# Attention into a causal gated unit on one core: k^T v over 128 rows, wide fillers, 7-product output blocks for two more batches, and a new order

## The chip, the cores and the metric

The kernel runs on one core of a Trainium2 chip. The time is device microseconds of one execution. A profile is one execution recorded by the hardware profiler, as times of every instruction from the start of the span. The engines: PE multiplies matrices (PEld is its loading of weights, which lies beside it), DVE (VectorE), ACT (ScalarE) and POOL (GpSimd) work element by element, SP issues DMAs; ACT and POOL issue some too.

## What is computed

```python
# q, k, v: (8, 8, 576, 64) float32: batch, heads, tokens, head size
kv  = einsum('bhsd,bhse->bhde', k, v)
out = einsum('bhsd,bhde->bhse', q, kv)
out = out / sqrt(mean(out * out, axis=-1) + 1e-6) * g_norm
x   = out.transpose(0, 2, 1, 3).reshape(8, 576, 512)
gate_pre[t] = sum over i in 0..4 of conv_w[i] * x[t - 4 + i]     # zeros ahead of the first token
gate = 1 / (1 + exp(-gate_pre))
result = (gate * (x @ w_val)) @ w_out       # w_val, w_out: (512, 512); conv_w: (5, 512); all three float64
```

There is no softmax: a 64x64 matrix k^T v for each head is all that attention needs of k and v.

## The kernel before

Everything is float32, and PE makes two passes of each matmul. The eight batches run through the same steps, and the steps of neighbouring batches are interleaved. There is no loop around them: PLAN is a text of 1103 steps, each a function with its arguments, carried out from first to last when the program is built. Its order is therefore the order of every engine's own queue; an engine that waits holds up all that stands behind it in its queue.

The steps of a batch b:

- load_half (L290) loads half of the heads of k or v, 576 KB, as 128 partitions (s, the parity of the head, times 64 groups p of nine tokens), for two heads g each: nine tokens of 64 numbers in a row, 2304 contiguous bytes. Batch 0's v goes by ACT's queue, the rest by SP's; batch 1's lies in slots 1 and 2 of gv, which are free then; other batches have one buffer for each half. load_q (L300) loads a pair of heads as four DMAs of 32 partitions; batches 0 and 1 use load_q_rows (L309).
- kv_product (L417), a half at a time: nine tokens of the group x 2 heads r x 2 parities s, each a matmul of 64 rows (the groups) and 64 columns. Four of them, one for each of four heads, on the four quarters of the array, can be in flight. They collect in the two banks "raws", one for each s. kv_copy (L425) moves the sums onto the diagonal blocks of kv_bd.
- turn_q (DVE) or, for batches 0 and 1, turn_q_rows (PE, L451, tile qTps) and sort_q (ACT) transpose q. raw_product (L472) and raw_pair (L489, 64x64 products) multiply it with kv.
- square (ACT), sums (DVE, L515), powers (POOL, L521) and normalise (DVE for batch 0, else ACT, L533) make x; turn_x and keep_x, or from batch 2 turn_blocks (DVE, L561) and move_blocks (POOL's DMAs, L569), transpose it into xT; halo (POOL) copies the convolution's edge.
- gate_start (ACT), four gate_tap (DVE, L586) and gate_end (ACT) make the gate. x @ w_val is val_product (L598) for batches 0 and 1; from batch 2 it is val_fast (L648), seven products where eight would be needed, with x_sums (DVE) ahead of it and val_keep (ACT copies and DVE adds, L655 to L669) between. gated (DVE, L611) multiplies with the gate in place in gv, which has three slots, b modulo 3.
- The last product takes two batches at a time, i = b // 2. out_product i c (L679; L686 for the rest of both batches, c = 8) makes 128 tokens by 512 columns from four matmuls of 512 columns, and keep_out (ACT, L694) copies them. For i = 3 alone, two such blocks are one pair made of seven products of 2 matmuls by 256 columns: token_sums (DVE, L719), fast_product (L745), and fast_keep (four ACT copies, three DVE adds, L754 to L769). weight_sums (DVE, L702) prepares the weights for it once. store (L778) writes a block as four DMAs.
- narrow_weight turns float64 weights into float32, on DVE and ACT, eight steps a tile.

Buffers that set waits: PSUM has five banks "mm", one "tp" and two "raws"; val_fast takes three mm banks at once, a pair of fast_product two, an out_product one. Tile ot has three buffers, w64 (staged weights, later the token sums) three.

keep_warm (L408) is work for PE without use: matmuls of the identity with itself, 13 of them at the start and three at two places later.

Of the kernel before, what the change touches and what calls it, by code (L numbers as in the profile page):

```python
# [9 lines left out]
FP32 = mybir.dt.float32  # L10
# [5 lines left out]
P = 128  # L16
# [3 lines left out]
load_q_rows 0 1; stage_weight cw 0; load_q_rows 0 0; load_half v 0 0; load_half k 0 0; load_half v 0 1;  # L20
load_half k 0 1; warm_up; stage_weight wval 1; stage_weight wval 0; keep_warm 13; turn_q_rows 0 0;
turn_q_rows 0 1; sort_q 0 0; narrow_weight cw 0 0; turn_q_rows 0 2; sort_q 0 1; narrow_weight cw 0 1;
turn_q_rows 0 3; narrow_weight cw 0 2; narrow_weight cw 0 3; sort_q 0 2; turn_q_rows 0 4; narrow_weight cw 0 4;
kv_product 0 0; narrow_weight cw 0 5; sort_q 0 3; load_q_rows 1 0; narrow_weight cw 0 6; narrow_weight cw 0 7;
load_half k 1 0; sort_q 0 4; load_q_rows 1 1; load_half v 1 0; keep_warm 3; kv_product 0 1; load_half k 1 1;
stage_weight wval 2; keep_warm 3; turn_cw; load_half v 1 1; kv_copy 0; stage_weight wval 3; raw_product 0 3;
narrow_weight wval 0 0; raw_product 0 2; narrow_weight wval 1 0; square 0 3; keep_cw; narrow_weight wval 0 1;
raw_product 0 4; sums 0 3; raw_product 0 1; square 0 4; powers 0 3; square 0 2; narrow_weight wval 0 2;
raw_product 0 0; sums 0 2; narrow_weight wval 0 3; sums 0 4; powers 0 2; narrow_weight wval 1 1; normalise 0 3;
load_q 2 2; turn_q_rows 1 0; square 0 1; narrow_weight wval 0 4; square 0 0; sums 0 1; turn_x 0 3; sort_q 1 0;  # L30
powers 0 4; turn_q_rows 1 1; stage_weight wout 0; normalise 0 2; keep_x 0 3; narrow_weight wval 0 5;
turn_x 0 2; sums 0 0; powers 0 1; kv_product 1 0; normalise 0 4; keep_x 0 2; narrow_weight wval 0 6;
narrow_weight wval 1 2; narrow_weight wval 0 7; turn_x 0 4; narrow_weight wval 1 3; powers 0 0;
turn_q_rows 1 2; normalise 0 1; keep_x 0 4; sort_q 1 1; narrow_weight wval 2 0; turn_q_rows 1 3;
narrow_weight wval 1 4; sort_q 1 2; narrow_weight wval 1 5; kv_product 1 1; halo 0; narrow_weight wval 2 1;
normalise 0 0; sort_q 1 3; narrow_weight wval 1 6; turn_q_rows 1 4; kv_copy 1; narrow_weight wval 1 7;
turn_x 0 1; load_q 2 0; sort_q 1 4; narrow_weight wval 3 0; keep_x 0 1; raw_pair 1 3; narrow_weight wval 2 2;
turn_x 0 0; load_q 2 1; square 1 2; val_product 0 0 1; square 1 3; sums 1 2; keep_x 0 0; sums 1 3;
gate_start 0 0; load_half k 2 1; powers 1 2; narrow_weight wval 3 1; val_product 0 1 1; gate_tap 0 0 3;
narrow_weight wval 2 3; gate_tap 0 0 2; powers 1 3; normalise 1 2; narrow_weight wval 2 4; load_half v 2 0;  # L40
val_product 0 0 0; gate_tap 0 0 1; load_half k 2 0; stage_weight wout 2; gate_tap 0 0 0; load_half v 2 1;
normalise 1 3; narrow_weight wval 2 5; narrow_weight wval 2 6; turn_q 2 0; narrow_weight wval 3 2;
raw_pair 1 1; narrow_weight wval 2 7; gate_start 0 1; load_q 2 3; turn_q 2 1; turn_x 1 3; square 1 1;
val_product 0 1 0; square 1 0; sums 1 1; keep_x 1 3; gate_tap 0 1 3; keep_val 0 0 0; powers 1 1;
gate_start 0 3; sums 1 0; raw_product 1 4; keep_val 0 0 1; narrow_weight wout 0 0; narrow_weight wval 3 3;
turn_x 1 2; gate_tap 0 3 3; keep_val 0 1 1; val_product 0 2 1; powers 1 0; square 1 4; narrow_weight wval 3 4;
normalise 1 1; load_q 3 0; gate_tap 0 3 2; turn_q 2 2; val_product 0 2 0; stage_weight wout 1; normalise 1 0;
narrow_weight wval 3 5; gate_tap 0 1 2; narrow_weight wval 3 6; narrow_weight wout 0 1; narrow_weight wval 3 7;
kv_product 2 0; load_q 3 1; keep_x 1 2; sums 1 4; gate_end 0 0; gate_tap 0 1 1; powers 1 4; turn_x 1 1;
narrow_weight wout 0 2; gate_tap 0 3 1; keep_x 1 1; kv_product 2 1; gated 0 0; narrow_weight wout 0 3;  # L50
turn_q 2 3; keep_val 0 1 0; turn_x 1 0; kv_copy 2; gate_tap 0 1 0; load_q 3 2; normalise 1 4;
narrow_weight wout 0 4; raw_pair 2 3; keep_val 0 2 1; narrow_weight wout 0 5; keep_x 1 0;
narrow_weight wout 2 0; val_product 0 3 1; gate_tap 0 3 0; square 2 3; narrow_weight wout 2 1; sums 2 3;
square 2 2; turn_q 3 0; powers 2 3; gate_start 0 2; turn_x 1 4; val_product 0 3 0; sums 2 2;
narrow_weight wout 2 2; gate_tap 0 2 3; keep_x 1 4; narrow_weight wout 2 3; narrow_weight wout 0 6; powers 2 2;
normalise 2 3; val_product 1 0 1; narrow_weight wout 2 4; stage_weight wout 3; narrow_weight wout 0 7;
load_half k 3 0; gate_tap 0 2 2; load_half v 3 0; keep_val 0 3 1; halo 1; load_half v 3 1; normalise 2 2;
val_product 1 0 0; narrow_weight wout 1 0; load_q 3 3; turn_q 3 1; narrow_weight wout 2 5; keep_val 0 2 0;
gate_tap 0 2 1; narrow_weight wout 1 1; raw_pair 2 1; load_half k 3 1; narrow_weight wout 2 6; keep_val 1 0 1;
keep_val 1 0 0; turn_blocks 2 3; raw_product 2 4; keep_val 0 3 0; square 2 1; narrow_weight wout 2 7;  # L60
val_product 1 1 1; gate_end 0 1; sums 2 1; square 2 4; narrow_weight wout 1 2; narrow_weight wout 3 0;
powers 2 1; gate_tap 0 2 0; square 2 0; val_product 1 1 0; narrow_weight wout 1 3; sums 2 0; gate_end 0 2;
gated 0 1; narrow_weight wout 3 1; powers 2 0; load_q 4 0; sums 2 4; val_product 1 2 1; normalise 2 1;
narrow_weight wout 1 4; turn_blocks 2 2; gated 0 2; powers 2 4; normalise 2 0; val_product 1 2 0;
narrow_weight wout 1 5; turn_blocks 2 1; narrow_weight wout 1 6; gate_end 0 3; narrow_weight wout 1 7;
gate_start 1 0; kv_product 3 0; turn_blocks 2 0; keep_val 1 1 1; narrow_weight wout 3 2; gated 0 3;
val_product 1 3 1; normalise 2 4; turn_q 3 2; narrow_weight wout 3 3; turn_q 3 3; load_q 4 1; gate_start 1 2;
turn_x 2 4; narrow_weight wout 3 4; kv_product 3 1; keep_x 2 4; narrow_weight wout 3 5; keep_val 1 2 1;
move_blocks 2 3; gate_tap 1 0 3; keep_val 1 1 0; load_q 4 2; val_product 1 3 0; kv_copy 3;
narrow_weight wout 3 6; gate_tap 1 0 2; keep_val 1 3 1; load_half v 4 0; narrow_weight wout 3 7; raw_pair 3 3;  # L70
gate_tap 1 0 1; gate_tap 1 2 3; out_product 0 1; square 3 2; keep_val 1 2 0; sums 3 2; gate_start 1 3;
load_half k 4 0; gate_tap 1 0 0; square 3 3; powers 3 2; gate_tap 1 3 3; gate_end 1 0; sums 3 3;
out_product 0 2; gated 1 0; keep_out 0 1; powers 3 3; keep_val 1 3 0; gate_tap 1 3 2; gate_start 1 1;
gate_tap 1 2 2; normalise 3 2; gate_tap 1 1 3; move_blocks 2 2; gate_tap 1 1 2; out_product 0 3; keep_out 0 2;
gate_tap 1 3 1; normalise 3 3; store 0 2; gate_tap 1 1 1; halo 2; gate_tap 1 2 1; gate_tap 1 1 0;
load_half k 4 1; store 0 1; gate_tap 1 3 0; raw_pair 3 1; gate_end 1 1; gate_tap 1 2 0; keep_out 0 3;
move_blocks 2 1; raw_product 3 4; square 3 1; gated 1 1; out_product 0 0; gate_end 1 2; sums 3 1;
load_half v 4 1; square 3 0; gated 1 2; gate_end 1 3; powers 3 1; square 3 4; gated 1 3; store 0 3; turn_q 4 0;
sums 3 0; out_product 0 5; keep_out 0 0; load_q 4 3; weight_sums 0; powers 3 0; turn_blocks 3 3;
turn_blocks 3 2; val_sums 0; normalise 3 1; move_blocks 2 0; sums 3 4; out_product 0 7; val_sums 1;  # L80
normalise 3 0; turn_blocks 3 1; powers 3 4; turn_q 4 1; turn_q 4 2; load_q 5 0; normalise 3 4; weight_sums 1;
kv_product 4 0; val_sums 2; store 0 0; turn_x 3 4; turn_blocks 3 0; out_product 0 4; keep_x 3 4; turn_q 4 3;
keep_out 0 7; move_blocks 3 3; gate_start 2 0; val_sums 3; load_half v 5 0; keep_out 0 5; x_sums 2 0;
gate_start 2 1; x_sums 2 2; gate_start 2 2; gate_tap 2 0 3; kv_product 4 1; gate_tap 2 0 2; load_q 5 1;
val_fast 2 0 0; x_sums 2 1; kv_copy 4; x_sums 2 3; val_fast 2 0 1; load_half k 5 0; val_keep 2 0 0;
gate_tap 2 2 3; move_blocks 3 2; raw_pair 4 3; gate_tap 2 0 1; val_keep 2 0 1; keep_out 0 4; turn_q 5 0;
# [734 lines left out]
```

## Time and profile before

| | us |
|---|---|
| three timed runs | 322.24, 324.89, 323.32 (median 323.32) |
| the profiled execution | 320.15, of which the span is 318.4 |
| out_product L679, 192 passes | 85.7 busy, 0.594 each |
| raw in kv_product L417, 1008 + 144 passes | 18.5 + 2.9 busy |
| gate_tap L586, 128 on DVE | 101.7 busy |
| DMA | 55.50 MB, 174 GB/s in the mean |
| k, v loads from batch 2 on, issue to landing | 6.3 and 6.4 each of 576 KB |

A line of the page gives line, engine, operation, output tile and inputs, shapes and count, then the busy time and the mean duration of one. Busy times count overlaps once. A matmul's own duration includes its way through the array, so that a run of matmuls is priced by the distance of their starts, as the chain of waits lists it, not by the mean. "Issue" as a releaser means that nothing the profile shows ended the wait. The granted clock is full in every stretch of the page.

### The profile page before, as it was taken

How to read it: one execution, taken by the hardware profiler on the slowest of the kernel's cores; microseconds unless marked ns; L12 is line 12 of the kernel's file. 1: busy time of each engine (PE TensorE's matmuls, PEld its weight loads, DVE VectorE, ACT ScalarE, POOL GpSimd, SP SyncE). 2: the span in 40 equal slices, each digit the busy share in tenths (PEclk: the TensorE clock that was granted, in tenths of full speed). 3: DMA queues.
4: the chain of work that ended last, by engine and by line, in shares of the span. 5: the costliest groups of instructions: out<-in, count | busy, mean ns of one | idle time of the engine just before them, and what ended most of it. 6: DMA issues, size and time to landing. Idle time of an engine off the chain costs nothing.

```text
span 318.4 us, 8335 instructions
## 1 busy us (share of the span) xinstructions
PE 305.1 (96%) x3207; PEld 206.8 (65%) x3207; DVE 246.4 (77%) x431; ACT 191.4 (60%) x534; POOL 139.3 (44%) x177
## 2 busy tenths in 40 slices
PE   8797899999999999999999999999999999999994
PEld 7686667777644485676756676566666558884653
DVE  1159399999999979989998889989778794764402
ACT  2367799999586647775765776656863343323210
POOL 3038235456298637919552777297457000000000
PEclk9999999999999999999999999999999999999999
DMA  7998499597949898469768894432226041203233
GB/s 274 379 388 256 132 311 278 158 344 183 267 115 303 220 276 243 121 182 283 210 187 209 257 256 100 96 83 58 68 49 150 0 101 33 66 13 82 73 77 89
DMA packets 26696, 55.50 MB, mean 174 GB/s; under 512 B 6166, under 2 KB 8214, under 8 KB 26656
## 3 DMA queue, kind: packets, MB, share of 16 engines
q1 hardware_dynamic: 22608, 46.61, 50.8%
q0 software_dynamic: 3168, 6.32, 8.0%
q10 hardware_dynamic: 880, 2.03, 1.7%
q8 instruction: 25, 0.41, 0.6%
q14 instruction: 15, 0.12, 0.1%
HBM read 39.21 MB, written 9.44 MB: 153 GB/s over the span
## 4 chain that ended last, share of the span: by engine, by line
PE 88%; ACT 3%; issue 2%; DMA 2%; SPq 1%; DVE 1%; POOL 1%; POOLq 0%; ACTq 0%; DVEq 0%
PE out L679 26%; PE va L648 15%; PE vc L648 7%; PE raw L417 6%; PE val L598 6%; PE out L686 5%; PE raw L489 4%; PE a L745 4%; PE vb L648 4%; PE cb L745 3%; PE qTps L451 2%; PE warm L408 2%; PE raw L472 2%; DMA k<-in_k_dram 2%; SPq L300 1%
## 5 line engine op out<-in xcount | busy, mean ns | idle before, releaser
L586 DVE SCALAR_TENSOR_TENSOR gate<-xT,cwT,gate 128x576 f32<-128x576 f32 x128 | 101.7, 813 | 5.1 <-ACT gate L580 4.0
L521 POOL TENSOR_TENSOR rt<-ss,mhalf 128x8 f32<-128x8 f32 (+1 forms) x40 | 69.1, 1736 | 77.5 <-DVE ss L515 76.1
L679 PE MATMUL out<-wout,gv 128*128 128x512 f32 x192 | 85.7, 594 | 0.0
L569 POOL DMA_DIRECT2D xT<-y x96 | 53.1, 559 | 27.3 <-issue 8.7
L679 PEld LDWEIGHTS out<-wout,gv 128*128 128x128 f32 x192 | 36.1, 190 | 39.7 <-issue 37.6
L533 ACT ACTIVATE x<-raw,rt 128x64 f32<-128x64 f32 x252 | 55.4, 369 | 7.3 <-POOL rt L521 5.8
L515 DVE TENSOR_REDUCE ss<-sq 128x8 f32<-128x520 f32 (+1 forms) x40 | 24.8, 629 | 14.8 <-ACT sq L507 14.7
L598 PE MATMUL val<-xT,wval 128*128 128x288 f32 x128 | 32.8, 409 | 0.0
L611 DVE TENSOR_TENSOR gv<-gv,gate 128x576 f32<-128x576 f32 x32 | 23.7, 747 | 7.3 <-ACT gv L669 4.8
L593 ACT ACTIVATE gate<-gate 128x576 f32<-128x576 f32 x32 | 22.7, 710 | 9.5 <-DVE gate L586 9.3
L507 ACT ACTIVATE sq<-raw 128x512 f32<-128x512 f32 (+1 forms) x40 | 22.3, 575 | 9.8 <-PE raw L489 7.3
L694 ACT COPY ot<-out 128x512 f32<-128x512 f32 x28 | 16.3, 590 | 19.7 <-PE out L679 13.4
L598 PEld LDWEIGHTS val<-xT,wval 128*128 128x128 f32 x128 | 23.7, 190 | 6.3 <-issue 0.2
L648 PE MATMUL va<-xs,vsum 128*128 128x288 f32 x96 | 27.3, 407 | 0.0
L580 ACT ACTIVATE gate<-xT,cwT 128x576 f32<-128x576 f32 x32 | 25.2, 804 | 1.7 <-DVE gv L611 1.7
L417 PEld LDWEIGHTS raw<-v,k 64*64 64x64 f32 x1008 | 16.3, 134 | 9.7 <-issue 7.7
L648 PEld LDWEIGHTS va<-xs,vsum 128*128 128x128 f32 x96 | 18.2, 190 | 5.4 <-issue 0.5
L417 PE MATMUL raw<-v,k 64*64 64x64 f32 x1008 | 18.5, 221 | 2.9 <-issue 2.8
L489 PEld LDWEIGHTS raw<-kvbd,qT 64*64 64x64 f32 x896 | 14.3, 134 | 7.2 <-issue 2.9
L754 DVE TENSOR_TENSOR ot<-cb,ot 128x256 f32<-128x256 f32 x8 | 3.4, 424 | 17.9 <-ACT ot L758 14.9
L489 PE MATMUL raw<-kvbd,qT 64*64 64x64 f32 x896 | 16.3, 221 | 0.9 <-ACT x L533 0.6
L561 DVE STREAM_TRANSPOSE y<-x 128x512 f32<-128x512 f32 x24 | 16.7, 700 | 0.0
(110 smaller groups left out, 437.0 us busy)
## 6 DMA issues: line engine op xcount, KB each, us to landing
qs<-in_q_dram SPq DMA_DIRECT2D x96, 140.0 KB, 4.6
out_dram<-ot SPq DMA_DIRECT2D x140, 64.0 KB, 1.7
k<-in_k_dram SPq DMA_DIRECT2D x14, 576.0 KB, 6.3
v<-in_v_dram SPq DMA_DIRECT2D x12, 576.0 KB, 6.4
xT<-y POOLq DMA_DIRECT2D x96, 64.0 KB, 3.0
y<-in_moe_w_val_dram SPq DMA_DIRECT2D x4, 512.0 KB, 12.3
w_wout<-in_moe_w_out_dram SPq DMA_DIRECT2D x4, 512.0 KB, 6.2
qs<-in_q_dram SPq DMA_DIRECT2D x3, 576.0 KB, 7.7
```

Of the source, the lines that this page charges most:

```text
L417: nc.tensor.matmul(raws[r * D:(r + 1) * D, s, i * D:(i + 1) * D], st["k", b, i][rows, r, cols], st["v", b, i][rows, r, cols], start=(j == ...
L489: nc.tensor.matmul(st["raw", b, x][cols, r, hp * D:(hp + 1) * D], st["qT", b][rows, hp, x * P + half * D:x * P + (half + 1) * D], kv_bd[b ...
L515: nc.vector.reduce_sum(out=ss[:, 0:n], in_=st["sq", b, c][:, 0:n], axis=AX.X)
L521: nc.gpsimd.tensor_tensor(out=rt[:, 0:n], in0=st["ss", b, c][:, 0:n], in1=mhalf[:, 0:n], op=ALU.pow)
L533: nc.scalar.activation(out=x[:, to * D:(to + 1) * D], in_=one, func=AF.Copy, scale=st["rt", b, c][:, h:h + 1])
L569: nc.gpsimd.dma_start(out=xTs[b % 2][i * TB:(i + 1) * TB, :, first:first + P], in_=y[a * TB:(a + 1) * TB, i])
L580: nc.scalar.activation(out=gate[:], in_=xTs[b % 2][:, jt, HALO:SX], func=AF.Copy, scale=cwT[:, K - 1, jt:jt + 1])
L586: nc.vector.scalar_tensor_tensor(out=gate[:], in0=xTs[b % 2][:, jt, tap * TB:tap * TB + S], scalar=cwT[:, tap, jt:jt + 1], in1=gate[:], op ...
L598: nc.tensor.matmul(val[:], wval[:, kc, jt * P:(jt + 1) * P], xTs[b % 2][:, kc, HALO + n * SV:HALO + (n + 1) * SV], start=(kc == 0), stop=( ...
L611: nc.vector.tensor_tensor(out=both, in0=both, in1=st["gate", b, jt][:], op=ALU.mult)
L648: nc.tensor.matmul(st[bank, "val", b, mj][:], weights_[:, k], tokens()[:, k], start=(n in (0, 1, 3) and k == 0), stop=(k == NK // 2 - 1), ...
L679: nc.tensor.matmul(po[:], gv[:, jt, first:first + P], wout[:, jt, :], start=(jt == 0), stop=(jt == NK - 1),)
```

## The change

- k and v are loaded by another split of the tokens. A head's 576 tokens lie on 64 groups of nine; partitions 0 to 63 take the first four tokens of each group, partitions 64 to 127 the last five. A half (i) has the four heads 2m + i. A load is two DMAs, one for each set of partitions; the plan of batch 0 issues its two parts apart, part 0 on SP and part 1 on ACT. Batch 1's data lie over the first part of gv, its slot 0 included.
- kv_product makes, for each head, four matmuls of 128 rows and 64 columns (the tokens 0 to 3 of both sets of partitions) and a fifth of 64 rows (the ninth token, partitions 64 to 127). Two heads are on the two column halves. It uses one bank. There are 20 matmuls a half instead of 36.
- keep_warm multiplies the identity with kv_bd[1] (zeros at that time), 512 columns, two at the start and two later; start_warm is the old narrow one, five at the start after them.
- Batches 4 and 5 (i = 2) get fast_product, fast_keep and token_sums in place of eight out_product and keep_out: 28 products, 28 keeps and 8 sums more.
- All of PLAN is in a new order, 1155 steps. val_sums begin earlier, weight_sums stand further apart, load_q_rows and turn_q_rows of batch 1 come ahead of most of batch 0's raw_product.

```diff
+    RUN = (NJ + 1) * D
+    KV = H // 2 * RUN
-    def load_half(name, b, i):
-        src = (k if name == "k" else v)[b].rearrange("(g s) (p j) d -> (s p) g (j d)", s=2, j=NR)[:, i::2]
-        if b == 1:
-            first = (1 if name == "k" else 2) * S
-            t = gv[:, i::2, first:first + S]
-        else:
-            t = loads.tile([P, 2, NR * D], FP32, tag=f"{name}{i}", bufs=1, name=f"{name}{i}_{b}")[:]
-        (nc.scalar if b == 0 and name == "v" else nc.sync).dma_start(out=t, in_=src)
-        st[name, b, i] = t
+    def load_half(name, b, i, part):
+        if (name, b, i) not in st:
+            if b == 1:
+                st[name, b, i] = gv[:].rearrange("p k n -> p (k n)")[:, KV * (2 * "kv".index(name) + i):][:, 0:KV].rearrange(
+                    "p (m e) -> p m e", m=H // 2)
+            else:
+                st[name, b, i] = loads.tile([P, H // 2, RUN], FP32, tag=f"{name}{i}", bufs=1, name=f"{name}{i}_{b}")[:]
+        src = (k if name == "k" else v)[b].rearrange("(m i) (g j) d -> i g m (j d)", i=2, j=NR)[i]
+        for x in (part,) if b == 0 else range(2):
+            tokens = slice(0, NJ * D) if x == 0 else slice(NJ * D, NR * D)
+            (nc.scalar if part else nc.sync).dma_start(
+                out=st[name, b, i][x * D:(x + 1) * D, :, 0:(NJ + x) * D], in_=src[:, :, tokens])
...
+    def warm_bank():
+        if "warm" not in st:
+            st["warm"] = ps("tp", [P, HP, P], "warm")
+        return st["warm"]
+    def start_warm(n):
+        for _ in range(n):
+            nc.tensor.matmul(warm_bank()[:, 0], ident[:], ident[:], start=True, stop=True)
     def keep_warm(n):
-        if "warm" not in st:
-            st["warm"] = ps("tp", [P, P], "warm")
         for _ in range(n):
-            nc.tensor.matmul(st["warm"][:], ident[:], ident[:], start=True, stop=True)
+            nc.tensor.matmul(warm_bank()[:], ident[:], kv_bd[1][:], start=True, stop=True)
     def kv_product(b, i):
-        for j in range(NR):
-            for r in range(2):
-                for s in range(2):
-                    rows, cols = slice(s * D, (s + 1) * D), slice(j * D, (j + 1) * D)
+        kl, vl = st["k", b, i], st["v", b, i]
+        for n in range(2):
+            hp = i + 2 * n
+            for j in range(NJ + 1):
+                rows, cols = slice(D if j == NJ else 0, P), slice(j * D, (j + 1) * D)
+                for r in range(2):
                     nc.tensor.matmul(
-                        raws[r * D:(r + 1) * D, s, i * D:(i + 1) * D],
-                        st["k", b, i][rows, r, cols], st["v", b, i][rows, r, cols],
-                        start=(j == 0), stop=(j == NR - 1))
+                        raws[r * D:(r + 1) * D, 0, hp * D:(hp + 1) * D], kl[rows, 2 * r + n, cols], vl[rows, 2 * r + n, cols],
+                        start=(j == 0), stop=(j == NJ), skip_group_check=True)
     def kv_copy(b):
         for r in range(2):
             rows = slice(r * D, (r + 1) * D)
             nc.scalar.copy(
-                out=kv_bd[b % 2][rows, :, rows].rearrange("p (i s) e -> p s i e", s=2),
-                in_=raws[rows, :, 0:2 * D].rearrange("p s (i e) -> p s i e", i=2))
+                out=kv_bd[b % 2][rows, :, rows], in_=raws[rows, 0, 0:HP * D].rearrange("p (h e) -> p h e", h=HP))
```

The start of PLAN, before and after:

```diff
-load_q_rows 0 1; stage_weight cw 0; load_q_rows 0 0; load_half v 0 0; load_half k 0 0; load_half v 0 1;
-load_half k 0 1; warm_up; stage_weight wval 1; stage_weight wval 0; keep_warm 13; turn_q_rows 0 0;
...
-kv_product 0 0; narrow_weight cw 0 5; sort_q 0 3; load_q_rows 1 0; narrow_weight cw 0 6; narrow_weight cw 0 7;
-load_half k 1 0; sort_q 0 4; load_q_rows 1 1; load_half v 1 0; keep_warm 3; kv_product 0 1; load_half k 1 1;
+load_q_rows 0 1; stage_weight cw 0; load_q_rows 0 0; load_half k 0 0 1; load_half k 0 1 0; load_half v 0 0 1;
+load_half v 0 0 0; load_half k 0 1 1; load_half k 0 0 0; load_half v 0 1 1; warm_up; stage_weight wval 1;
+load_half v 0 1 0; keep_warm 2; start_warm 5; turn_q_rows 0 0; stage_weight wval 0; turn_q_rows 0 1; narrow_weight cw 0 0;
...
+narrow_weight cw 0 7; load_q_rows 1 0; sort_q 0 2; keep_warm 2; turn_cw; load_q_rows 1 1; sort_q 0 3; kv_product 0 0;
+stage_weight wval 2; load_half v 1 0 0; stage_weight wval 3; narrow_weight wval 1 0; keep_cw;
+narrow_weight wval 1 1; load_half k 1 0 0; kv_product 0 1; narrow_weight wval 1 2; sort_q 0 4;
```

The end of PLAN afterwards, where the two kinds of work that i = 2 got and the last products of i = 3 stand:

```diff
+val_keep 7 1 5; val_fast 7 1 6; fast_keep 3 1 0; gate_tap 7 1 0; fast_product 2 3 6; val_keep 7 1 6;
+gate_end 7 1; fast_product 3 1 1; fast_keep 2 3 6; gated 7 1; store 2 7; fast_product 3 1 2; gated 7 3;
...
+fast_product 3 2 6; fast_keep 3 2 5; store 3 4; fast_product 3 3 0; fast_keep 3 2 6; fast_product 3 3 1;
```

## Prediction, made before the changed kernel was run

> **What bounds the kernel now.** I read the busy times first, then the busy times by stage, then the chain of waits, then the DMA queues.
>
> ```profile
> span 318.4 us, 8335 instructions
> PE 305.1 (96%) x3207; PEld 206.8 (65%) x3207; DVE 246.4 (77%) x431; ACT 191.4 (60%) x534; POOL 139.3 (44%) x177
> ```
>
> PE is busy 305.1 of 318.4 us, so a change pays only if it takes work from PE or fills the 13.3 us in which PE is idle. The view by stretches (us from the start; PE, PEld, DVE, ACT, POOL busy; granted clock; DMA share; GB/s) says where those are:
>
> ```profile
> 8.00:16.00 8.00, 5.74 (x189) 5.17 (x187) 1.19 (x5) 2.89 (x7) 0.00 (x0) 1.00 1.07 380
> ...
> 24.00:32.00 8.00, 5.87 (x160) 4.92 (x161) 7.89 (x15) 5.62 (x11) 6.36 (x8) 1.00 0.87 250
> 32.00:40.00 8.00, 6.89 (x132) 5.68 (x132) 2.94 (x5) 5.95 (x13) 2.28 (x2) 1.00 0.47 136
> 40.00:50.00 10.00, 9.40 (x108) 7.17 (x107) 9.93 (x18) 9.81 (x34) 4.55 (x3) 1.00 0.98 316
> 50.00:60.00 10.00, 9.08 (x233) 7.09 (x233) 9.96 (x20) 9.62 (x29) 1.87 (x3) 1.00 0.89 258
> ```
>
> The reader is to see that PE's holes lie before 60 us. From 60 to 300 every stretch has PE full; about 4.3 us of tail after the last product (314.1 us) stay. The chain of waits shows what the holes are, and gives prices (start us, duration us):
>
> ```profile
> 10.42 1.21 PE raw L417 x72
> ...
> 12.52 0.92 PE raw L417 x46
> 13.44 2.24 issue
> ...
> 29.54 0.72 PE raw L417 x34
> 30.26 2.85 issue
> ...
> 55.03 0.51 issue
> ```
>
> All three holes stand inside kv_product (L417), and nothing the profile shows released PE after them. The queue table names the suspect:
>
> ```profile
> q8 instruction: 25, 0.41, 0.6%
> ```
>
> 0.41 MB for PE's 2 x 3207 weight loads and matmuls is 64 bytes each, so a packet brings 256 of them, 128 passes (one fp32 matmul is two passes). From the timeline I count 222 passes before the first hole and 253 between the first and the second, two packets' worth. The packet records put fetches at 13.13 to 14.28 and 30.42 to 31.58 us, and PE starts again 1.40 and 1.53 us after each landed. So 64x64 products, a pass every 17 ns, eat instructions faster than they come: 2.24 + 2.85 + 0.51 = 5.6 us.
>
> **The change, part by part.**
>
> *Instruction fetches: -5.6 us.* A half of kv_product goes from 72 passes to 40 and PE's total to about 2720 pairs. In the new order passes 95 to 222, the block ahead of the first hole, hold kv 0 0, kv 0 1, two full raw products (2.0 us) and 32 qTps passes (1.9 us): with kv_copy (0.75 us) at least 7.3 us for a fetch that took 5.75 us from entering its block to PE's restart the first time and 6.9 the second. I take all three holes as gone; at worst the second length returns in part, so the bounds are -2.7 and -5.6.
>
> *kv_product: +8.2 us, bounds +1.9 and +8.2.* Before, four 64x64 tiles run side by side, 18 rounds a half. Now two tiles of 128 rows x 64 columns run side by side: 20 rounds. A round costs the same: raw_pair (x64, 16 rounds, 1.09 us in the lines below) and kv_product (x72, 18 rounds, 1.21) differ by 0.12 us, 0.06 a round, which leaves 0.13 for starting and finishing a run of one shape; the 128-row, 64-column shape of qTps with twice the columns takes 4.36 us for 36 rounds, 0.12 each, half of it 0.06. So 20 rounds are 1.20 us. But the ninth token's product has 64 rows, so a half is now four runs (8, 2, 8, 2 rounds) with three changes of shape inside. That a change of shape costs, the chain shows:
>
> ```profile
> 113.94 0.97 PE vc L648 x4
> 114.91 1.09 PE raw L489 x64
> 116.00 1.17 PE va L648 x4
> ```
>
> The same four passes take 0.97 after their like and 1.17 after raw_pair: 0.13 + 0.20 for two changes, 0.165 each. Four runs are 1.20 + 4 x 0.13 = 1.72 us a half against 1.21, +0.51, times 16 = +8.2. If rows 64 to 127 alone go on without a change, it is 1.33, +0.12, +1.9. No row has 128 rows followed by 64 in the same columns; the nearest, qTps (128x64) into kv_product at 10.42, takes the full 1.21, as after 128x128 work, so I take the upper end. [...]
>
> *Shape changes elsewhere: -1.8 us.* In PE's order I count 82 changes of shape before and 71 afterwards, those inside kv_product left out (kv halves now often stand together, and end in raw_pair's shape): 11 x 0.165.
>
> *7-product blocks for batches 4 and 5: -3.2 us.* Eight blocks of L679 become four pairs of 28 passes.
>
> ```profile
> 259.84 3.43 PE out L679 x8
> ...
> 279.02 0.86 PE a L745 x4
> ```
>
> Two blocks are 6.87 us; 28 passes at 0.865/4 are 6.06. Four pairs save 4 x 0.81 = 3.2. Within a pair run without other work between, the sixth product waits for an add behind a copy: it starts 0.48 us after the pass ahead of it at 301.9 and at 312.1 us, where 0.22 is the pace. Two such pairs become three: +0.3. DVE gets 8 sums at 0.69 and 12 adds at 0.42, 10.6 us, ACT 16 copies at 0.37 for 8 at 0.59, +1.2. Between 200 and 300 us DVE is busy 74.9 us and ACT 45.5, so the cover is 25 us of idle DVE time; if a sum comes late, PE waits as long. The sums' three buffers now carry eight tiles, so the third sum of pair 2 1 waits for that pair's third product, and batch 6's taps queue behind it on DVE; in the order that product stands well ahead. A pair (2 banks) and val_fast (3) fill the five banks.
>
> *Fillers: +0.7 us.* The first 26 passes (4.65 us) become 4 of 512 columns and 10 of 128. They need kv_bd[1] zeroed, which DVE ends at 2.06 us, while ident came at 1.3. In the trace the first passes start 0.21 us apart, and 0.11 from 4.7 us on: the clock opens there. The wide passes (0.43 in L679, so 0.86 before) end between 4.9 and 7.6 us; I take 6.8 against q's arrival at 6.06. The later 12 passes (1.8 us) become 4 wide ones (1.7): nothing.
>
> *Loads.* SP issues 28 more DMAs of some 0.43 us: 12 us over the run, hidden by SP's own waits (76.6 us on ot copies alone); a store behind one comes 0.4 us later. ACT issues five at the start instead of three, its table load moves from 2.2 to about 3.2, ahead of its first copy at 7.4. Batch 1's k and v now lie over batch 0's part of gv, so keep_val of batch 0 waits for kv_product 1, which stands before the first val_product anyway. At nothing, then, unless the transfers themselves slow down (second rival).
>
> **Sum.** -5.6 + 8.2 - 1.8 - 3.2 + 0.3 + 0.7 = -1.4 us. [...] The profiled execution takes 320.15 us, span and what lies around it: 318.7 afterwards. It was quicker than all three timed runs; on their median, 323.32, the forecast is 321.9.
>
> **Rivals.**
> *Shape inside kv_product costs nothing.* For it: all 128 rows and the lower 64 share a column half, and nothing else differs. Against: qTps into kv_product. Then 6.3 us more are saved: 315.6.
>
> *Half the partitions, slower loads (the other side).* A load of k or v for a later batch is now two DMAs, one to partitions 0 to 63, then one to 64 to 127. For it: in the packet records, 4480-byte packets of q, to 32 partitions a DMA, take 253 ns in the median, 4608-byte ones to 128 partitions 182; per byte 2304-byte k/v packets to 128 partitions take 0.040 ns and the 32-partition ones 0.057, 1.4 times. A half load is 256 packets of 117 ns on 16 engines, 1.9 us; 0.4 of it on the eight loads of batches 1 and 2 is 6 us, where the DMA share is 1.07, 1.05 and 0.87 up to 32 us and 0.98 and 0.89 from 40 to 60. Against: 32 to 40 us has 4.2 us of free DMA time, and later loads have a whole batch of lead. If it decides, PE waits for v of batch 1 or the weights behind it: -1.4 + 6 = +4.6, 327.9. It turns the sign from 0.2 us a load on.
>
> **How the numbers follow.** Forecast 0.45 (319 to 325), first rival 0.33, second 0.17, 0.05 for anything else, such as DVE coming late with sums. One per cent, 3.2 us, is about what a measurement of this kernel can tell from no change. Faster by more: 0.93 of the first rival, a sixth of the forecast: 0.38. Slower: most of the second, a little of the forecast and the rest: 0.22. Within: 0.40. The range takes in both rivals with the bounds of the fetches and fillers: 314 to 328.
>
> **What would show it.** No hole of over 1 us on PE before 60 us; the 14 kv halves of batches 1 to 7 at 1.7 us each, not 1.3; the first val_product 1 to 2 us earlier than 36.6; the last eight pairs at 6.1 us; no PE wait on k, v or sums. Wrong if kv halves take 1.3 us, if a hole stays, or if PE waits for DMA or DVE after 40 us.

## The result, and the profile after

| | us |
|---|---|
| the changed kernel, four runs | 331.16 to 332.03, median 331.41 |
| the kernel before, four runs beside it | 321.06 to 324.89, median 322.78 |
| ratio | 1.0267, interval 1.0202 to 1.0332 |
| the profiled execution of the changed kernel | 331.16, of which the span is 329.4 |

Medians are over all runs; ratios leave out runs in a slower state, over 1.5% above the fastest of their kernel. The forecast was 321.9 in a range of 314 to 328; the time lies above the range, and above the rival on the slow side (327.9) too. The busy times of the page after (engine, busy us, share, instructions):

```profile
span 329.4 us, 7463 instructions
...
PE 315.1 (96%) x2723; PEld 224.6 (68%) x2723; DVE 254.6 (77%) x451; ACT 192.1 (58%) x542; POOL 135.2 (41%) x177
```

PE has 484 pairs of instructions less than before and is busy 10 us longer. The view by stretches (same columns as before: us; PE, PEld, DVE, ACT, POOL; granted clock; DMA share; GB/s) shows one reason: from 16 us on the clock is granted at half for part of the time (16.5 to 26.8 and 37.0 to 43.8 us), and a slow pass counts as busy: those of raw_product (L494) start 0.21 us apart from 21 to 24 us, and 0.11 from 32.2 to 33.0, at the full clock.

```profile
8.00:16.00 8.00, 7.31 (x107) 5.45 (x103) 1.43 (x6) 3.59 (x9) 0.00 (x0) 1.00 1.10 289
16.00:24.00 8.00, 6.36 (x56) 5.86 (x56) 1.08 (x5) 3.88 (x7) 0.00 (x0) 0.53 1.08 324
24.00:32.00 8.00, 8.00 (x96) 7.26 (x96) 6.36 (x12) 5.92 (x11) 4.84 (x3) 0.83 1.12 233
32.00:40.00 8.00, 4.96 (x78) 4.25 (x78) 5.77 (x11) 3.42 (x8) 4.71 (x6) 0.81 1.10 245
...
50.00:60.00 10.00, 9.37 (x109) 7.15 (x108) 9.99 (x18) 9.62 (x35) 5.40 (x3) 1.00 1.04 246
```

The last two columns show the other. Before, the DMA engines moved 380 GB/s at a share of 1.07 from 8 to 16 us, and from 32 to 40 they had spare time (0.47). Now their share is at 1.08 to 1.12 all the way to 40 us, while the rate falls to 233 and 245 GB/s: as busy as before, they move a third less. The chain of waits of the changed kernel (start us, duration us) follows the transfers, not PE:

```profile
2.93 9.53 DMA k<-in_k_dram
...
12.90 13.48 DMA gv<-in_v_dram
...
26.41 11.79 DMA gv<-in_v_dram
...
38.33 3.00 PE raw L441 x40
...
86.20 3.51 PE raw L441 x80
...
303.82 0.86 PE a L767 x4
...
306.46 1.13 PE cb L767 x4
```

The queue of instruction fetches answers to the row of before that had 25 packets:

```profile
q8 instruction: 21, 0.34, 0.5%
```

gv holds batch 1's k and v. kv_product 1 1 starts at 38.33 us, where it started at 29.47 before. The view of waits (engine and line, what it waits for: us in total, times, longest) has the wait for it:

```profile
PE raw L441 <- DMA gv<-in_v_dram: 3.0, 1, 3.0
PE warm L432 <- DVE kvbd L277: 2.2, 1, 2.2
PE raw L441 <- issue: 1.4, 1, 1.4
```

The row "issue" is also a transfer, though the page names none: the hole lies from 15.37 to 16.79, and a part of v that kv_product 0 1 needs was issued at 8.3 us; these parts take 8.5 us to land. Milestones on PE, from the two traces: the first product of q at 7.22 us (before 6.06), kv_product 1 0 at 33.46 (26.00), the first val_product at 44.56 (36.60), the last pass 10.9 us later than before. So 8 of the 11 us between the two profiles are lost ahead of the first val_product, and the rest behind it.

### The profile page after: what moved, and what is told of

Its sections match the earlier page's. It is cut to its first block, busy times and chain, and to the rows that moved or that the text cites. A ratio compares the mean times of both kernels' runs of the same rounds, so it can differ in the third digit from the quotient of the medians.

```text
span 329.4 us, 7463 instructions
## 1 busy us (share of the span) xinstructions
PE 315.1 (96%) x2723; PEld 224.6 (68%) x2723; DVE 254.6 (77%) x451; ACT 192.1 (58%) x542; POOL 135.2 (41%) x177
## 4 chain that ended last, share of the span: by engine, by line
PE 81%; DMA 11%; ACT 4%; SPq 1%; issue 1%; DVE 1%; ACTq 0%
PE out L701 17%; PE va L670 14%; PE val L620 8%; DMA gv<-in_v_dram 8%; PE raw L441 7%; PE a L767 7%; PE vc L670 7%; PE cb L767 6%; PE raw L511 5%; PE out L708 4%; PE vb L670 4%; DMA k<-in_k_dram 3%; ACT x L555 1%; PE xTps L570 1%; PE raw L494 1%
## 5 line engine op out<-in xcount | busy, mean ns | idle before, releaser
L701 PE MATMUL out<-wout,gv 128*128 128x512 f32 x128 | 56.4, 594 | 0.0
L701 PEld LDWEIGHTS out<-wout,gv 128*128 128x128 f32 x128 | 24.2, 190 | 27.7 <-issue 26.5
L529 ACT ACTIVATE sq<-raw 128x512 f32<-128x512 f32 (+1 forms) x40 | 21.6, 562 | 17.3 <-PE raw L511 10.1
L441 PE MATMUL raw<-v,k 128*64 128x64 f32 (+1 forms) x560 | 26.3, 237 | 1.4 <-issue 1.4
L441 PEld LDWEIGHTS raw<-v,k 128*64 128x64 f32 (+1 forms) x560 | 21.8, 142 | 7.2 <-issue 2.9
L511 PEld LDWEIGHTS raw<-kvbd,qT 64*64 64x64 f32 x896 | 15.0, 140 | 7.7 <-issue 3.1
L776 DVE TENSOR_TENSOR ot<-cb,ot 128x256 f32<-128x256 f32 x16 | 6.8, 422 | 14.1 <-ACT ot L780 7.0
L716 ACT COPY ot<-out 128x512 f32<-128x512 f32 x20 | 12.1, 612 | 8.7 <-PE out L708 5.1
```

Source lines behind the costliest of these rows:

```text
L441: nc.tensor.matmul(raws[r * D:(r + 1) * D, 0, hp * D:(hp + 1) * D], kl[rows, 2 * r + n, cols], vl[rows, 2 * r + n, cols], start=(j == 0), ...
L511: nc.tensor.matmul(st["raw", b, x][cols, r, hp * D:(hp + 1) * D], st["qT", b][rows, hp, x * P + half * D:x * P + (half + 1) * D], kv_bd[b ...
L701: nc.tensor.matmul(po[:], gv[:, jt, first:first + P], wout[:, jt, :], start=(jt == 0), stop=(jt == NK - 1),)
```

## The experiments

Theory **L**: a DMA to half of the partitions runs at about half the rate, and what the front (the work up to some 45 us) loses is that. Theory **S**: the changes of shape inside kv_product cost what the prediction took. The rivals are that short rows, the number of DMAs, the order, or the half clock (theory C) make the front late. Medians of the kernel before are those of its runs on the same chip beside the run told of. Runs 1 to 4, 5 to 8, 9 to 11, and 12 and 13 are four groups, each on a chip of its own, and the changed kernel was not timed again beside them. So a difference to the changed kernel is given twice where it matters: of the medians, and of the two ratios to the kernel before, which take the chip out.

**1. Short rows alone.** The kernel before, each load of k and v cut by tokens.

```diff
-        (nc.scalar if b == 0 and name == "v" else nc.sync).dma_start(out=t, in_=src)
+        for cut in (slice(0, NJ * D), slice(NJ * D, NR * D)):
+            (nc.scalar if b == 0 and name == "v" else nc.sync).dma_start(out=t[:, :, cut], in_=src[:, :, cut])
```

> The kernel before, with each load of k or v cut by tokens into two DMAs over all 128 partitions: rows of 1024 and 1280 bytes instead of 2304, as short as in the changed kernel, and as many DMAs. Theory L (the two DMAs to half of the partitions each deliver k and v too slowly): within 2 us of before, packets of 1024 bytes near 50 ns as in the weight loads of before. Rival R (short rows or more DMAs are what is slow): 5 to 8 us slower, with PE waiting for v of batch 1.

Measured 321.76 against 324.93, ratio 0.992 (0.987 to 0.997). In the packet records rows of 1024 and 1280 bytes take 47 and 56 ns in the median (SP's queue, up to 60 us; the 1024-byte rows of the weights are among them). Neither the shorter rows nor twice the DMAs cost anything. The run is 3.2 us quicker, where within 2 us was expected; why is not shown.

**2. Half the partitions alone.** The kernel before, its rows of 2304 bytes as they are, each load cut by partitions.

```diff
+        for half in (slice(0, D), slice(D, P)):
+            (nc.scalar if b == 0 and name == "v" else nc.sync).dma_start(out=t[half], in_=src[half])
```

> The kernel before, with each load of k or v cut into two DMAs of unchanged rows of 2304 bytes, one to partitions 0 to 63, one to 64 to 127. Theory L: packets of 2304 bytes go from 95 ns to about 150 and the run is 3 to 8 us slower before 60 us. Rivals R and O (the new order puts too much ahead of v of batch 1): within 2 us of before.

Measured 333.92, ratio 1.029 (1.024 to 1.034): 9 us for a change that alters no instruction of PE and no byte. That is more than the 3 to 8 us expected. A packet of 2304 bytes takes 179 ns instead of 95 (medians from 8 to 40 us), where about 150 was expected. Its waits and two of its stretches:

```profile
PE raw L418 <- DMA k<-in_k_dram: 5.9, 4, 3.5
PE raw L418 <- DMA gv<-in_v_dram: 3.4, 2, 2.7
```

```profile
8.00:16.00 8.00, 5.83 (x138) 5.18 (x134) 1.19 (x5) 4.40 (x10) 0.00 (x0) 1.00 1.06 217
...
32.00:40.00 8.00, 5.71 (x131) 4.73 (x130) 4.48 (x9) 5.14 (x10) 4.34 (x6) 1.00 1.10 220
```

The signature is that of the changed kernel, a full DMA share at 217 and 220 GB/s. In the changed kernel itself 1280-byte packets to partitions 64 to 127 take 101 ns (SP's queue, up to 60 us), against 56 to all partitions in the run above; those of 1024 bytes to partitions 0 to 63 take 84 from 28 to 36 us, against 47. The price shows only in a stream: in run 2, where loads begin after a pause (at 140.1 and 154.9 us), the first 128 packets still take 93 ns, and those behind them 155 to 182 (medians of 64 at a time). Why a transfer to half of the partitions takes so long is not shown.

**3 and 4. The two halves of the change, crossed.** The order, fillers and blocks of before with the new loads and kv_product, and the reverse: the new PLAN, fillers and blocks with the old load_half, kv_product and kv_copy.

```diff
-load_half v 0 0; load_half k 0 0;
+load_half v 0 0 0; load_half v 0 0 1; load_half k 0 0 0; load_half k 0 0 1;
```

> The order, fillers and output blocks of before, with the loads and kv_product of the changed kernel. Theory S (changes of shape: a half of kv_product takes 1.75 us instead of 1.21) with L: 8 to 14 us slower, 6.5 of it from batches 2 to 7 at 0.54 a half. Rival O (the order is what costs): at most 3 us slower, as PE gets the same waits as before. Fetch holes of 2.24 and 2.85 us shrink in both.

> The order, fillers and output blocks of the changed kernel, with the loads and kv_product of before. S and L: 316 to 321 us, since 3.2 us go with the output blocks and a fetch hole may come back. Rival O: 326 us or more, with PE still waiting for v of batch 1 near 30 us or later.

Measured 331.71 (ratio 1.023, 1.018 to 1.028) for the new loads and products in the old order, where PE waits 4.7 us for q, which stands behind the slow loads in SP's queue; and 320.90 (0.987, 0.981 to 0.993) for the new order with the old loads and products. The first is 6.8 us slower, less than the 8 to 14 expected for S with L and more than the 3 of rival O; the second lies in the 316 to 321 expected. The order, the fillers and the blocks are no loss; loads and kv_product are. In the second, with 64x64 products back, three holes without a releaser stand in them again:

```profile
PE raw L440 <- issue: 6.0, 3, 3.7
```

**5. One DMA a head over all partitions.** An attempt to mend the changed kernel's loads from batch 1 on: rows of five tokens, a source with a stride for the two sets of partitions and one for the groups.

```diff
+            both = bass.AP(rows.tensor, rows.offset, [[NJ * D, 2]] + [list(p) for p in rows.ap])
+            nc.sync.dma_start(out=st[name, b, i][:, m, :], in_=both)
```

> The changed kernel, but from batch 1 on a half of k or v comes as four DMAs, one a head, each to all 128 partitions, with rows of five tokens (partitions 0 to 63 get the group's fifth token too, which no product reads there). Batch 0's loads stay as they are, in two queues at once. It moves about 11% more bytes of k and v. Theory L (a DMA to 64 partitions runs at half the rate, and that is what the front loses): 1280-byte packets take some 56 ns, as with two DMAs to all partitions, not 101; the wait of 3.0 us for batch 1's v is gone or under 1 us, the first val_product comes 3 to 6 us earlier than 44.6, and the time is 324 to 328. Rival (the order or the clock makes the front late, not the rate): 330 to 333.

Measured 617.73 us, nearly twice the time, which neither theory foresaw. The timeline of SP (start, us, what, count) shows the loads one at a time:

```profile
12.63 12.82 SPq L307 DMA_DIRECT2D gv<-in_v_dram  x4
...
28.80 25.29 SPq L307 DMA_DIRECT2D gv<-in_k_dram  x8
```

One DMA of 128 packets takes SP 3.2 us. The DMA share is 0.13 from 54 to 68 us, as much as two of the 16 engines would make if they alone were busy; an estimate from these numbers, 64 packets of the measured 55 ns on each of two engines, is 3.5 us. Why so little of the DMA engines is in use is not shown. The test says nothing on theory L: its 1280-byte packets take 55 ns, but at a share of 0.13.

**6. No change of shape inside a half.** The fifth product with 128 rows like the others; what it leaves out of the sum is nothing, since the fifth token of partitions 0 to 63 is zero.

```diff
-                rows, cols = slice(D if j == NJ else 0, P), slice(j * D, (j + 1) * D)
+                rows, cols = slice(0, P), slice(j * D, (j + 1) * D)
```

> The changed kernel, but the fifth product of each head has 128 rows like the other four; the fifth token of partitions 0 to 63 is zero (the buffers of k and v are fixed and cleared once by POOL, batch 1's place in gv as well). Theory S (three changes of shape inside a half cost 0.42 us together): from start to start a half goes from 1.75 to about 1.33 us, and twelve halves of batches 2 to 7, where PE is full, give 5 us: 325 to 328, though what is ahead of 45 us stays as late as it is. Rival (128 rows by 64 columns are dear by themselves, or the two heads do not run side by side): a half stays at 1.7, 330 to 333.

Measured 324.75 (323.90 to 327.72), 6.7 us below the changed kernel (7.6 by the ratios), ratio to before 1.003 (1.000 to 1.007). In the chain of waits two halves together go from 3.51 us (line 86.20 above) to 2.48:

```profile
87.45 2.48 PE raw L446 x80
```

That is 1.03 us for seven changes of shape, three inside each half and one between the two: 0.15 each. Halves that stand alone go from 1.75 to 1.32 us, 0.43 for three. The start times of the passes show that it is the change that costs and not the products of 64 rows: in the changed kernel the first pass of the other shape starts 0.15 us after the last one, in both directions, and the two passes behind it 0.10 us later, where 0.05 is usual. The first val_product is still at 43.68 us. S holds, at the price that the prediction took.

**7. The waits filled.** Six wide fillers ahead of the three waits.

```diff
-kv_product 0 1;
+fill 2; kv_product 0 1;
...
-raw_product 0 3;
+fill 1; raw_product 0 3;
...
-kv_product 1 1;
+fill 3; kv_product 1 1;
```

> The changed kernel with six wide fillers (512 columns, 0.86 us each at the full clock) ahead of three steps at which PE waits: two ahead of kv_product 0 1 (1.4 us of wait), one ahead of raw_product 0 3 (0.8), three ahead of kv_product 1 1 (3.0). Theory C (the clock halves after such waits, from 16.5 to 26.8 and from 37.0 to 43.8 us, and the work behind runs at half speed): the clock stays full, the first val_product comes 3 us or more earlier, 325 to 328. Theory L alone (data are late whatever PE does): the fillers take the place of the waits, the first val_product stays within 1 us of 44.6, 330 to 333.

Measured 330.51 (330.33 to 330.97). Its stretches:

```profile
16.00:24.00 8.00, 8.00 (x91) 5.69 (x89) 1.09 (x4) 4.71 (x10) 0.00 (x0) 1.00 1.08 322
24.00:32.00 8.00, 7.00 (x90) 6.11 (x85) 7.68 (x16) 6.75 (x15) 6.33 (x4) 1.00 1.12 233
32.00:40.00 8.00, 5.75 (x74) 3.62 (x76) 3.85 (x8) 1.23 (x4) 3.22 (x6) 1.00 1.10 239
```

The clock is now full throughout, and the rates are those of the changed kernel, 322, 233 and 239 GB/s. The waits are not all gone: from 31.0 us PE waits 2.54 us for k of batch 1 ahead of kv_product 1 0, and no half clock follows. The first val_product comes at 43.10 us, 1.5 earlier, between the two expectations, but the last pass only 0.5 earlier; the median is 0.9 lower (2.5 by the ratios, 1.019 against 1.027). The half clock is a follower of the late data, and what it costs by itself is small against the 7 to 9 us that the loads cost. Theory C falls as the main cause; its 325 to 328 was not reached.

**8. The fillers alone, in the kernel before.**

```diff
-keep_warm 13; turn_q_rows 0 0;
+keep_warm 2; start_warm 5; turn_q_rows 0 0;
...
-keep_warm 3;
+keep_warm 1;
```

> The kernel before with the changed kernel's fillers alone: two wide and five narrow ones at the start for thirteen, one wide for three at the two later places. By the prediction's term the first product of q starts 0.7 us later, and the time is about that much longer, 323 to 325. If the clock opens later or its holes then fall otherwise, as in the changed kernel (6.3 us for 4.5), the holes in kv_product may be followed by a half clock and the time is 325 to 328.

Measured 320.69, ratio 0.988 (0.985 to 0.992): 3.8 us less, where the prediction had 0.7 more. It is the same gain, to 0.2 us, as the new order, fillers and blocks have together in run 4: nothing of the time shows that order and blocks add to it.

**9 and 10. Two queues.** The changed kernel, and the one of run 6, with the part for partitions 64 to 127 of batches 1 and 2 issued by ACT.

```diff
-            (nc.scalar if part else nc.sync).dma_start(
+            (nc.scalar if part or (x and b in (1, 2)) else nc.sync).dma_start(
```

> The changed kernel, but for batches 1 and 2 the part of a load for partitions 64 to 127 is issued by ACT, so that it can run beside the part for partitions 0 to 63 in SP's queue; bytes, rows and products are the same. Theory L (it is the transfers to half of the partitions, one set after the other in one queue, that halve the rate): from 16 to 40 us more than 300 GB/s, the wait of 3.0 us for batch 1's v is gone or moved, the first val_product comes 4 to 7 us earlier than 44.6, 324 to 328. Rival L2 (rows of 1024 and 1280 bytes to 64 partitions are slow in any mixture, or ACT, which has to reach the DMA in its own order, issues them late): the same rate of 230 to 250 GB/s from 24 us on, 330 to 333.

> The same two queues, with the fifth product of 128 rows as in the run that priced it (buffers cleared once). If the two losses are independent, its gain of 6.7 us comes on top of whatever the two queues bring: 317 to 321 if they bring 4 to 7, below both kernels. If the front alone decides, because PE is late there whatever a half costs, no more than 325.

Measured 330.32 and 324.94 (ratios 1.024 and 1.006, against 1.027 and 1.003 without): no clear gain. Of L's expectation the wait for batch 1's v is gone, but waits of 1.0 and 0.8 us are put down to q, and the first val_product comes at 42.02, 2.5 us earlier and not 4 to 7. Rival L2's expectation came true in the time; two stretches of run 9:

```profile
24.00:32.00 8.00, 6.50 (x92) 5.68 (x90) 4.07 (x8) 4.36 (x9) 3.34 (x3) 1.00 1.12 258
32.00:40.00 8.00, 5.90 (x98) 4.97 (x98) 7.89 (x15) 5.17 (x11) 6.21 (x7) 1.00 1.10 242
```

In the packet records both sets of partitions are written at once only in part. From 25 to 27 us, where packets of both queues lie side by side, the DMAs move 291 and 292 GB/s, and 181 to 216 from 29 to 32, where no packet of ACT's queue is in flight; but from 32 to 36, with both again, it is 216 to 229. A full rate is not reached even beside each other; why is left open.

**11. The kernel before, another profile.**

> The kernel before as it is, to see another profile of it: that of the prediction was quicker than every timed run. If a hole in kv_product falls otherwise against the steps in which the clock is granted, a stretch of half clock follows it, as in the runs with the changed fillers, and the span is some us above 318.4; if the clock is full throughout again and the span within 1 us of 318.4, the gain of the fillers alone stays unexplained.

Measured 325.86 with a span of 324.1, 5.7 us longer than the profile that the prediction read. Its wait and two stretches:

```profile
PE raw L417 <- issue: 7.3, 3, 3.1
```

```profile
32.00:40.00 8.00, 6.93 (x127) 5.67 (x127) 1.40 (x3) 4.58 (x10) 0.84 (x1) 0.79 0.47 129
...
50.00:60.00 10.00, 6.57 (x162) 5.11 (x161) 9.96 (x20) 7.15 (x23) 3.81 (x3) 1.00 0.84 225
```

The three holes inside kv_product stand behind the same passes in both profiles, the 222nd, 475th and 857th; they are 1.52, 3.12 and 2.67 us here, where the first profile had 2.24, 2.85 and 0.51, and two stretches of half clock of 3.41 us follow them, at 33.5 and 60.8 us. The spans of the same program thus lie 5.7 us apart. The holes are 1.7 us longer in sum, and a stretch of half clock of 3.41 us can cost 1.7 (an estimate, half of its length), so that the holes and what follows them can account for most of it. Beside it, run 8's profile has holes of 1.32 and 2.01, again behind passes 222 and 475, no third one, and one such stretch: with 20 passes taken out of the front, the same counts fall on later steps of the program. That this is the whole of its gain is not shown: it rests on one profile, whose span of 319.1 us lies above the first profile of before (318.4) and below the second.

**12 and 13. Full rate by another split of the tokens.** The changed kernel; the first 512 tokens of a head lie four on each of all 128 partitions, the last 64 one each on partitions 64 to 127. Products and sums are the same. Then the same with run 6's 128 rows.

```diff
+        src = (k if name == "k" else v)[b].rearrange("(m i) s d -> i s m d", i=2)[i]
-                out=st[name, b, i][x * D:(x + 1) * D, :, 0:(NJ + x) * D], in_=src[:, :, tokens])
+                out=st[name, b, i][x * D:P, :, x * NJ * D:(NJ + x) * D],
+                in_=src[P * NJ:] if x else (k if name == "k" else v)[b].rearrange("(m i) s d -> i m (s d)", i=2)[i][
+                    :, 0:P * NJ * D].rearrange("m (p e) -> p m e", p=P))
```

> The changed kernel, its products as they are, with another split of the tokens: the first 512 tokens of a head lie four on each of all 128 partitions (one DMA a half, 1024-byte rows), the last 64 one each on partitions 64 to 127 (a second DMA of 256-byte rows, 64 KB). The sums are over the same tokens. Theory L (transfers to 64 partitions run at half the rate and make the front late): 1024-byte packets take about 47 ns, from 8 to 24 us some 370 GB/s, no wait over 1 us for batch 1's k or v, the first val_product 4 to 8 us ahead of 44.6, 322 to 326. Rival (it is the order, the waits in PE's queue or the number of DMAs): 330 to 333. The 256-byte rows may cost more than I think; then the rate shows it.

> The same split, with the fifth product of 128 rows (fifth token of partitions 0 to 63 zero, buffers cleared once), so that no shape changes inside a half. If both losses are what the runs so far say, 6.7 us less than the run before: 315 to 319, ahead of both kernels and of the two versions at 320.7 to 320.9. If the front stays late, 324 to 326.

Measured 322.80 (322.11 to 325.97) and 316.66 (315.88 to 317.02). The first is 8.6 us below the changed kernel (7.2 by the ratios), ratio to before 1.004 (0.999 to 1.010). The second, on the same chip, is another 6.1 below; the ten halves in pairs and two alone of batches 2 to 7, at the prices of run 6, make 6.0. Its ratio is 0.984 (0.977 to 0.991): faster than before, though not surely by 2%. Against the versions of runs 4 and 8 (0.987 and 0.988) no gain is shown. The stretches of run 12:

```profile
8.00:16.00 8.00, 7.94 (x125) 6.16 (x123) 2.17 (x9) 4.80 (x10) 0.00 (x0) 1.00 1.13 333
16.00:24.00 8.00, 7.16 (x112) 6.33 (x108) 3.05 (x6) 5.66 (x11) 2.07 (x2) 1.00 1.07 358
24.00:32.00 8.00, 7.22 (x110) 6.30 (x108) 7.89 (x16) 5.79 (x12) 6.35 (x5) 1.00 1.13 311
32.00:40.00 8.00, 7.74 (x116) 6.29 (x116) 5.03 (x11) 6.67 (x16) 4.42 (x7) 1.00 0.96 228
```

and its waits for batch 1's data:

```profile
PE raw L442 <- DMA gv<-in_v_dram: 0.8, 1, 0.8
```

The transfers move 311 to 358 GB/s where the changed kernel had 233 to 324, and their share is back under 1 before 40 us. The wait of 3.0 us is 0.8, the clock stays full, the first val_product starts at 35.59 us, 9.0 earlier, and the last pass 9.0 earlier too: what the front gains reaches the end undiminished. The 1024-byte packets take 49 ns, the 256-byte ones 18. The rate falls a little short of the 370 GB/s that were expected.

## Why the prediction was wrong

**The step that failed** is the one on loads: "At nothing, then, unless the transfers themselves slow down (second rival)." They do, and the term is +7 to +9 us (run 12 against the changed kernel: 7.2 by the ratios, 8.6 by the medians, 9.0 between the last passes of the profiles), not nothing. The prediction had named the mechanism, and then went wrong in three places of the second rival.

- *The price of a load.* It took 1.4 from q, loaded by DMAs of 32 partitions, as the factor for k and v. Measured by themselves, 2304-byte packets go from 95 to 179 ns, 1.9 times. With 0.9 of the 1.9 us in place of 0.4, its own sum for eight loads gives 13.7 us, and the 4.2 us of free DMA time that it set against them bring that to 9.5, near what was measured.
- *The cover.* The 4.2 us between 32 and 40 us were real, and were used up: the DMA share there went from 0.47 to 1.10. They were a reserve of a few us against three times that (13.7), not an argument for no loss.
- *The chance.* 0.17 was too little for a mechanism that a row of the trace spoke for directly. Its place was right: batch 1's k and v, on the way to the first val_product.

A small reading on loads was off too: SP got 30 more DMAs of k and v (60 for 30), not 28, and one takes it some 0.6 us, not 0.43; ACT's table load came at 7.0 us, not 3.2. No wait shown above is put down to either.

**The other terms** add up less well than their sum looks: without the slow loads (run 12) the ratio to before is 1.004 (0.999 to 1.010), where the forecast without the second rival is 0.996. That is some 3 us, and which of the terms below it belongs to is not shown.

- *kv_product, +8.2:* right. A half takes 1.75 us (3.51 for two) against a predicted 1.72. The chain of reasoning stands too: a change of shape costs 0.15 us, where 0.165 was read from val_fast's rows, and a half without changes takes 1.32 where 1.33 was taken. The first rival (shape costs nothing, 315.6) falls.
- *Fetch holes, -5.6:* holes without a transfer behind them are gone; in run 12 no pause inside kv_product is longer than 0.8 us, and that one is a transfer. But the term had been read from one execution in which they were cheap: in the second profile of before they are 7.3 us, with two stretches of half clock behind them.
- *Fillers, +0.7:* the first product of q comes later by more than that (7.82 us in run 8 against 6.76 in run 11 and 6.06 in the first profile). The time fell by 3.8 all the same, where the holes had moved. Fillers and fetch holes were added as if they were independent; run 8 shows that fillers decide which steps the holes fall on.
- *7-product blocks, -3.2 + 0.3:* the pace (0.86 us a product) came as computed, and so did the pauses in three pairs: the passes at 306.46, 316.66 and 323.08 start 0.44 to 0.49 us after the one ahead, 0.22 being the pace. No run took the blocks away alone, and *shape changes elsewhere, -1.8,* was not tried by itself either. Run 4 has blocks, order and fillers, run 8 fillers alone, and their ratios differ by 0.1%, with 0.4 to 0.6% of uncertainty each: a gain of 2.9 us from the blocks does not show there.

Of the signs that the prediction set for itself, "no PE wait on k, v or sums" and "the first val_product 1 to 2 us earlier than 36.6" failed, at 3.0 us and at 44.56, and so did "no hole of over 1 us on PE before 60 us", at 3.04 and 1.42; all pointed at the loads. In run 12 the first val_product comes at 35.59, and no hole there is over 1 us.

## What to carry to other kernels

A DMA's share of busy time does not tell its rate: a load split into two sets of 64 partitions kept the share at 1.06 and 1.07 in run 2 and moved 217 and 289 GB/s from 8 to 24 us, where 380 and 388 had been, so price it by the packet's duration, in a stream and in a run of that very shape, before calling it hidden. A free stretch in a queue is a reserve with a size, to be set against the whole added time. And before pricing holes that depend on where instruction blocks fall, look at a second execution: the third hole took 0.51 us in one and 2.67 in another. An edit elsewhere moves them too, as 20 passes less did here.

## What was not expected of the hardware

- Half of the partitions: 2304-byte packets took 179 ns against 95, and 1280-byte ones 101 against 56, though the first 128 packets after a pause took 93 as before.
- Two queues, each with one half of the partitions, moved 216 to 292 GB/s beside each other (run 9), not the 380 of loads to all partitions.
- A change between 128x64 and 64x64 products cost 0.15 us (1.03 us for seven).
- The loads of run 5, 160 KB each over all partitions from a source with a stride for the two sets of partitions, took 3.2 us of SP's time each at a DMA share of 0.13, and the kernel 617.73 us.
- The granted clock fell to half for stretches of 3.41 us, or a multiple, in or after pauses of PE of some 1.2 to 3.7 us (in the changed kernel from 16.5 to 26.8 us at a pause of 1.42, and from 37.0 to 43.8 at one of 3.04), but not with each: before's holes of 2.24 and 2.85 us left it full in one execution and two of three were followed by a half clock in another (run 5 aside, where pauses are longer).
- Fillers kept the clock full (run 7, 1.00 in each stretch shown), and the last pass came 0.5 us earlier, since the data were late anyway.
